# Gated mix of linear attention and a gated ReLU network on one core: six slots for the output row tiles, query weights folded beside key weights, GpSimd's main loop in program order

## The chip, the cores and the metric

The kernel runs on one core of a Trainium2 chip. The metric is the time of one execution on the device in microseconds, the median over runs. The core's engines work in parallel, each through its own list of instructions in order: TensorE (PE in the profile, with its weight loads as PEld), VectorE (DVE), ScalarE (ACT), GpSimd (POOL), and SyncE (SP), which here only issues transfers. Transfers from SP and from GpSimd run on the same 16 DMA engines.

## The reference

Inputs are x (2048 rows of 576), float32. The output is a gate times an attention layer plus the rest of the gate times a feed-forward layer:

```python
qkv = (x @ wqkv).reshape(B, S, 3, H, Dh).transpose(2, 0, 3, 1, 4)    # H = 32 heads of Dh = 18
pq = einsum("bhsd,hdf->bhsf", q, w_phi); pk = einsum("bhsd,hdf->bhsf", k, w_phi)
phi_q = concat([softmax(pq), softmax(-pq)]); phi_k = concat([softmax(pk), softmax(-pk)])
kv = einsum("bhsf,bhsd->bhfd", phi_k, v); z = einsum("bhsf->bhf", phi_k)
o = einsum("bhqf,bhfd->bhqd", phi_q, kv) / (einsum("bhqf,bhf->bhq", phi_q, z) + 1e-6)
a = o @ wo
h = relu(x @ W_gate) * (x @ W_up);  b = h @ W_down                   # F = 4608
g = sigmoid((x * gate_w).sum(-1));  out = g * a + (1 - g) * b
```

## The kernel before

Products are made of float32r parts: a high part that ScalarE rounds (an activation with Copy) and a low part, source minus high, that VectorE subtracts (`split`, L148). So each product costs two or three matmuls.

**Stage 1, to about 31 us.** The values of the first four row tiles (L212 to L245). Then `fold` (L250) multiplies the key weights by the per-head matrix: 25 small matmuls into the three buffers `psf` of the pool `pf`, each group then split by ScalarE and VectorE into `wk_h` and `wk_l`. The weights arrive in tiles `wr` of the pool `raw`, which has four slots in all; a slot is used again when its reader is done, so the order of the loads is also the order in which slots come free.

**Stage 2, folding, to about 60 us.** L397 to L403: `fold` for keys, `load_x(1)` (the next 512 rows of x, tiles `xr`, split into `xh`, `xl`, `x4`), `keys(0)`, `keys(1)`, and `fold` for queries (`wq_h`, `wq_l`). `keys(t)` and `queries(t)` each project a tile of 128 rows by 28 matmuls into one of the two buffers of pool `pp` (`pk`, `pq`). VectorE then takes the maximum and minimum and makes the two differences (`mx`, `mn`, two `e`), which frees the buffer, ScalarE takes the exponential, VectorE the sums `sm` and a reciprocal. For a key tile VectorE scales one half of `e` and GpSimd the other; for a query tile GpSimd scales one half (`e<-r`, L210).

**Stage 3, the main loop, to about 250 us.** L460: for each of the tiles 2 to 13 the keys, the values of the tile (two halves into one PSUM bank `kv`), the queries, the transposes of an earlier query tile (`turn`, `ptr`), and 11 matmuls that add to the attention sums (`kv_step`). From t = 8 GpSimd also makes the first half of the feed-forward operands: `scaled_sums` (L324) loads four blocks `xb`, multiplies them by a row of roots `sb`, subtracts them from one another, and stores seven results to `xt` in device memory. `first_half` is a generator; L471 steps it five times ahead of each tile. Before the change it works on two halves of 256 columns one after the other (eight tiles `xb`). No order is written out in this loop: the tile framework's scheduler places each engine's instructions by its own estimate, within the data dependences.

**Stage 4, attention output, to about 367 us.** Four blocks of 512 rows, the last block first. For block b: `sums` (numerators and denominators, from operands `ph` that `fetch` loads from `eT`), `gather`, `invert` (the denominators `dn`, collected by small transfers on SP, inverted by VectorE, sent on to `kt`), `split_inverse` (GpSimd: `rd`), `divide` (one matmul that spreads `rd`, a VectorE product, then a split into `oh` and `ol`), and the projection: `first_out` for block 0, `project_out` for the others, 14 matmuls for each of five row tiles m. `rows_out` (L756) copies a finished row tile from PSUM to a tile `o` of the pool `tb` and stores it to `att`. For m = 4 the two halves of the bank have to be added: ScalarE copies one half to a tile `b`, VectorE adds the other into `o`. The pool `tb` has four slots, and m = 4 takes two of them; `root_rows` takes one for each of its two calls. Tensor, SP and GpSimd instructions of stages 4 and 5 are held in program order (`in_order`, L54).

**Stage 5, the feed-forward loop, from about 367 us to the end.** 72 units of seven products (`product`, L1091). `second_half` (L1209) makes the other half of the operands, one step per unit, with the same `scaled_sums`.

Of the kernel before, what the change touches and what calls it, by code (L numbers as in the profile page):

```python
# [2 lines left out]

# [13 lines left out]
P = 128  # L17
TB = 512
# [66 lines left out]
def gated_mix_kernel(  # L85
# [77 lines left out]
    def load_x(tb):  # L163
        s = slice(tb * TB, (tb + 1) * TB)
        xh, xl, x4 = x_tiles(tb)
        a = raw.tile([P, 3, TB], F32, name="xr", tag="raw")
        nc.sync.dma_start(a, xT[:, 0:3, s])
        split(xh[:, 0:3], xl[:, 0:3], a)
        b = raw.tile([P, 2, TB], F32, name="xr", tag="raw")
        nc.sync.dma_start(b, xT[:, 3:5, s])  # L170
        split(xh[:, 3], xl[:, 3], b[:, 0])
        split_x4(x4, b[:, 1])
# [77 lines left out]
    def fold(src, dst_h, dst_l, pf):  # L250
        for j0 in range(0, NF, 2):
            n = min(2, NF - j0)
            w = raw.tile([FG, 2, DK], F32, name="wr", tag="raw")
            nc.sync.dma_start(w[:, :n], src[:, j0:j0 + n])
            for j in range(j0, j0 + n):
                c0, gn = FOLDS[j]
                for d0, dn in ((0, 4), (4, 1)):
                    ps = pf.tile([P, 4, P], F32, name="psf")
                    for d in range(dn):
                        nc.tensor.matmul(ps[:, d, :gn], w[:gn, j - j0, (d0 + d) * P:(d0 + d + 1) * P],  # L260
                                         bd[:gn, j, :gn], start=True, stop=True)
                    split(dst_h[:, d0:d0 + dn, c0:c0 + gn], dst_l[:, d0:d0 + dn, c0:c0 + gn],
                          ps[:, :dn, :gn])
# [18 lines left out]
    def keys(t):  # L282
        for _ in key_steps(t):
            pass
# [13 lines left out]
    def whole(steps):  # L298
        for _ in steps:
            pass  # L300
# [16 lines left out]
    def on_all_rows(ps, dst, tb):  # L317

        for i in range(4):
            t = 4 * tb + i  # L320
            nc.tensor.transpose(ps[:, i * P:(i + 1) * P], rs[:, t:t + 1].to_broadcast([P, P]), ident)
        nc.scalar.activation(dst, ps, AF.Copy)

    def scaled_sums(f, hf, b, sb, c0, n):  # L324


        b11, b12, b21, b22 = b
        put = lambda i, a: nc.sync.dma_start(xt[:, hf, i - 1, :, c0:c0 + n], a)
        for i, a in enumerate(b):
            k, t = divmod(i, 2)  # L330
            nc.sync.dma_start(a, xs[:, k, :, (2 * hf + t) * TB + c0:(2 * hf + t) * TB + c0 + n])
        yield
        for i, a in enumerate(b):
            f(out=a, in0=a, in1=sb[:, i % 2, None, :].to_broadcast([P, 3, n]), op=MULT)
            yield
            if i != 1:
                put((1, 0, 2, 3)[i], a)
        for i, o, a, c in ((5, b11, b12, b11), (7, b12, b22, b12), (6, b22, b22, b11), (4, b21, b21, b22)):
            f(out=o, in0=a, in1=c, op=SUB)
            yield  # L340
            put(i, o)
        yield

    def query_steps(t, between=lambda: None, eng=nc.gpsimd):

# [15 lines left out]
    def queries(t):  # L361
        for _ in query_steps(t):
            pass
# [32 lines left out]
    ET = {}  # L396
    with tc.tile_pool(name="pf", bufs=3, space=PSUM, reuse_waits="tile") as pf:  # L397
        fold(wkT, wk_h, wk_l, pf)
        load_x(1)
        nc.sync.dma_start(ident, ident_d)  # L400
        keys(0)
        keys(1)
        fold(wqT, wq_h, wq_l, pf)  # L403
    gate_logits(0)
    gate_logits(1)
    ps_kv = AP.enter_context(tc.tile_pool(name="ps_kv", bufs=1, space=PSUM, reuse_waits="tile"))
# [16 lines left out]
    def operands(tb):  # L423
        PH[tb] = PP[BLOCKS.index(tb) % 2].tile([QK, 4, NQ, P], F32, name="ph")

# [17 lines left out]
            for i in range(0, 5, 2):  # L443
                nc.sync.dma_start(wod[i // 2, :, 10:12 if i < 4 else 11], o[:, 0, i:min(i + 2, 5)].bitcast(F32))

    xw = AR.enter_context(tc.tile_pool(name="xw", bufs=8, **R_))
    WOUT = {}

    def load_out_weights():
# [7 lines left out]
                WOUT[4, k] = w[:, 10 + k % 2], None  # L457

    first_half = iter(())
    for t in range(2, NT - 2):  # L460
        if t in (6, 10):
            load_x(t // 4 + 1)
        if t == 8:
            whole(half_gates(0))
            sb = xw.tile([P, 2, TB], F32, name="sb", bufs=1)
            for i in range(2):
                on_all_rows(pv1.tile([P, TB], F32, name="pg", tag="pv1"), sb[:, i], i)
            halves = [[xw.tile([P, 3, TB // 2], F32, name="xb") for _ in range(4)] for _ in range(2)]
            first_half = chain(*(scaled_sums(pt, 0, halves[c], sb[:, :, c * TB // 2:][:, :, :TB // 2], c * TB // 2, TB // 2)
                                 for c in range(2)))  # L470
        for _ in range(5):  # L471
            next(first_half, None)
        if t == 12:
            for _ in first_half:
                pass
            AR.close()
            pad = RS.enter_context(tc.tile_pool(name="pad", bufs=1, **R_))
            pad.tile([P, 24], F32, name="pad")
            kt_p = RS.enter_context(tc.tile_pool(name="kt_p", bufs=1, **R_))
            kt_ = kt_p.tile([P, 2 * TB], F32, name="kt")  # L480
            gT = kt_[:, TB:]
            kt = kt_[:, :NJ * QK].rearrange("p (g c) -> p g c", g=NJ)
            PP = [RS.enter_context(tc.tile_pool(name="ph0", bufs=1, **R_))]
            operands(BLOCKS[0])
            spread = kt_p.tile([4 * H, 5, P], F32R, name="spread")
            ones = raw.tile([4 * H, 5, P], F32, name="ones", tag="raw")
            nc.sync.dma_start(ones, spread_d)
            nc.gpsimd.tensor_copy(spread, ones)
            load_out_weights()
        keys(t)  # L490
        if t >= 4:
            turn(t - 4, 0)
            values(t, 0)
            turn(t - 4, 1)
            values(t, 1)
        gate_logits(t)
        queries(t - 2 if t < FIRST else t)
        if t >= 4:
            turn(t - 4, 2)
        kv_step(t - 2)  # L500
        if t in (2, 3, 4, 5, 7):
            out_weights((2, 3, 4, 5, 7).index(t))


    def kv_out():
        nc.scalar.activation(kt[:, 4:], kv[1][:, :NJ - 4], AF.Copy)
# [149 lines left out]
    with in_order(tc, nc, nc.tensor, nc.sync, nc.gpsimd):  # L656
# [51 lines left out]
        invert(0)  # L708
        gather(0, 3, 2, 1, 0)
        split_inverse(0)  # L710
        store_turned(FIRST - 2, nc.gpsimd)
        fetch(BLOCKS[2], nc.gpsimd)
        two = pp.tile([P, 2, TB], F32, name="po", tag="pp")
        sums(1, (4,), (kv_bank(0),))
        sums(1, (5,), (kv_bank(1),))
# [29 lines left out]
    xo = ctx.enter_context(tc.tile_pool(name="xo", bufs=3, **L_))  # L745
    xr = ctx.enter_context(tc.tile_pool(name="xr", bufs=2, **L_))
    op_ = BS.enter_context(tc.tile_pool(name="op", bufs=2, **L_))
    tb_ = BS.enter_context(tc.tile_pool(name="tb", bufs=4, **L_))
    XO = {}
    def root_rows(tb):  # L750

# [4 lines left out]
    def rows_out(b, m, ps):  # L756

        n = P if m < 4 else 64
        o = tb_.tile([n, TB], F32, name="o", tag="tb")
        if m < 4:  # L760
            nc.scalar.activation(o, ps, AF.Copy)
        else:
            c = tb_.tile([64, TB], F32, name="b", tag="tb")
            nc.scalar.activation(c, ps[64:], AF.Copy)
            tt(out=o, in0=c, in1=ps[:64], op=ADD)
        nc.sync.dma_start(att[m * P:m * P + n, BLOCKS[b] * TB:(BLOCKS[b] + 1) * TB], o)

    def project_out(b, m):
# [825 lines left out]
```

## Time and profile before

| | |
|---|---|
| three runs | 1623.77, 1625.07, 1628.36 us; median 1625.07 |
| the profiled execution | 1625.07 us, its span 1623.3 us, so 1.8 us lie around the span |
| busy share of the span | PE 98%, PEld 81%, DVE 74%, ACT 34%, POOL 11% |
| granted TensorE clock, mean | 0.991 of full |
| stages by the timeline | values and key weights to 31.6 us, folding to 60.2, main loop to about 250, attention output to 367.0, feed-forward to the end |

A row of the view by windows gives a stretch (start and end in us from the span's start), its length, then for each engine the busy time and the number of instructions, the granted clock, the DMA engines' busy share and GB/s. A row of a timeline gives start, duration, engine, line, operation, output and input tiles with their shapes, how many instructions are merged, and in brackets how long the engine stood idle before and what it waited for. Matmuls overlap, so the recorded duration of one is longer than its step to the next. A row of the view of waits gives who waited for whom, the total, how often, and the longest.

### The profile page before, as it was taken

The page shows a single profiled execution, that of the slowest core. Times are in us where ns is not written, and L with a number is a line of the kernel's source. Part 1 is how long each engine was busy: PE and PEld are TensorE (multiplying, and loading weights), DVE is VectorE, ACT ScalarE, POOL GpSimd, SP SyncE. Part 2 cuts the span into 40 slices and gives each one's busy share as a digit, 9 for nine tenths or more (in the row PEclk, how much of TensorE's full clock was granted, in tenths as well). Part 3 has the DMA queues.
Part 4 walks back from the last instruction along what each step waited for, and adds up shares of the span by engine and source line. Part 5 has one row for each costly group of instructions (what it writes and reads, how often), then busy time and mean ns, then how long its engine had stood idle before and what let it go on. Part 6 is the DMA issues. An engine that isn't in the chain of part 4 may idle for free.

```text
span 1623.3 us, 20196 instructions
## 1 busy us (share of the span) xinstructions
PE 1587.4 (98%) x7823; PEld 1319.7 (81%) x7823; DVE 1195.4 (74%) x1864; ACT 559.9 (34%) x918; POOL 171.7 (11%) x234
## 2 busy tenths in 40 slices
PE   8999999898999999999999999999999999999998
PEld 8899996466888888888888887788888888888887
DVE  4898775368777877877777777677777777767777
ACT  4344335345323323323323324232323223232331
POOL 0128311200000000000000002111111111111110
PEclk9899999999999999999999999999999999999999
DMA  8254405557675566566555434643434334353432
GB/s 269 66 187 135 147 17 148 185 202 281 227 259 222 195 224 248 189 225 230 194 197 194 186 120 152 223 167 134 180 129 180 147 148 166 132 192 131 165 149 73
DMA packets 71562, 284.59 MB, mean 175 GB/s; under 512 B 7018, under 2 KB 25962, under 8 KB 62764
## 3 DMA queue, kind: packets, MB, share of 16 engines
q1 hardware_dynamic: 69020, 273.30, 46.5%
q0 software_dynamic: 1872, 8.97, 1.9%
q8 instruction: 61, 1.00, 0.3%
q10 hardware_dynamic: 576, 1.05, 0.2%
q14 instruction: 33, 0.27, 0.0%
HBM read 172.67 MB, written 109.21 MB: 174 GB/s over the span
## 4 chain that ended last, share of the span: by engine, by line
PE 88%; DVE 4%; DMA 3%; POOL 2%; ACT 1%; issue 1%; SPq 0%; DVEq 0%; POOLq 0%; ACTq 0%
PE cx L1091 27%; PE ca L1091 13%; PE pd L1131 12%; PE pd L1154 10%; PE cy L1091 7%; PE kv L176 4%; PE pq L176 3%; PE pk L176 2%; PE pm L1131 2%; PE pm L1154 2%; PE pw L176 1%; PE kv L416 1%; DMA wdr<-wd 1%; PE pv L238 1%; DMA ph<-eT 1%
## 5 line engine op out<-in xcount | busy, mean ns | idle before, releaser
L1198 ACT ACTIVATE hh<-g 128x512 fp32r<-128x512 f32 x195 | 120.0, 624 | 459.0 <-DVE g L1248 289.7
L1169 DVE TENSOR_TENSOR ac<-pd,ac 128x512 f32<-128x512 f32 x238 | 163.9, 689 | 146.3 <-PE pd L1154 146.1
L1091 PE MATMUL cx<-xo,ws 128*128 128x512 f32 x1008 | 253.3, 391 | 4.2 <-ACT g L1252 4.2
L1091 PE MATMUL cx<-xo,wb 128*128 128x512 f32 x1008 | 250.9, 392 | 5.2 <-DVE u L1373 3.5
L1091 PE MATMUL ca<-xo,ws 128*128 128x512 f32 x1008 | 252.0, 389 | 0.7 <-DMA ws<-wsd 0.7
L1091 PEld LDWEIGHTS cx<-xo,wb 128*128 128x128 f32 x1008 | 189.2, 189 | 47.3 <-DVE u L1373 4.3
L1091 PEld LDWEIGHTS cx<-xo,ws 128*128 128x128 f32 x1008 | 189.5, 188 | 44.8 <-ACT g L1252 5.4
L1091 PEld LDWEIGHTS ca<-xo,ws 128*128 128x128 f32 x1008 | 189.1, 188 | 40.3 <-issue 1.1
L1131 PE MATMUL pd<-hh,wd 128*128 128x512 f32 x576 | 200.7, 389 | 0.0
L1154 PE MATMUL pd<-hh,wd 128*128 128x512 f32 x476 | 185.2, 389 | 0.0
L1137 DVE TENSOR_TENSOR ac<-pd,ac 128x512 f32<-128x512 f32 x144 | 99.0, 688 | 106.6 <-PE pd L1131 103.1
L1203 DVE TENSOR_TENSOR hl<-g,hh 128x512 fp32r<-128x512 f32 x195 | 136.3, 699 | 1.9 <-ACT hh L1198 0.2
L1252 ACT ACTIVATE g<-cx 128x512 f32<-128x512 f32 x144 | 85.0, 590 | 127.1 <-PE cx L1091 127.0
L1091 PE MATMUL cy<-xo,wb 128*128 128x512 f32 x504 | 126.6, 391 | 0.0
L1131 PEld LDWEIGHTS pd<-hh,wd 128*128 128x128 f32 x576 | 108.1, 188 | 22.5
L1054 ACT ACTIVATE wd<-wdr 128x384 fp32r<-128x384 f32 (+1 forms) x106 | 62.3, 606 | 153.4 <-DMA wdr<-wd 153.4
L1131 PE MATMUL pd<-hl,wd 128*128 128x512 f32 x288 | 112.1, 389 | 1.0 <-ACT xo L823 1.0
L1091 PEld LDWEIGHTS cy<-xo,wb 128*128 128x128 f32 x504 | 95.2, 189 | 20.0
L1154 PEld LDWEIGHTS pd<-hh,wd 128*128 128x128 f32 x476 | 89.3, 188 | 18.6
L1154 PE MATMUL pd<-hl,wd 128*128 128x512 f32 x238 | 92.6, 389 | 0.0
L807 POOL TENSOR_TENSOR xo<-xr,xo 32x512 fp32r<-32x512 f32 x5 | 8.2, 1638 | 656.2 <-DVE xo L807 648.4
L1057 DVE TENSOR_TENSOR wd<-wdr,wd 128x384 fp32r<-128x384 f32 (+1 forms) x106 | 69.4, 669 | 5.7 <-ACT wd L1054 5.7
(250 smaller groups left out, 2577.8 us busy)
## 6 DMA issues: line engine op xcount, KB each, us to landing
wsd<-ws SPq DMA_DIRECT2D x34, 1280.0 KB
ws<-wsd SPq DMA_DIRECT2D x34, 1280.0 KB
wbd<-wb SPq DMA_DIRECT2D x34, 960.0 KB
wb<-wbd SPq DMA_DIRECT2D x34, 960.0 KB
wr<-wgu SPq DMA_DIRECT2D x36, 768.0 KB
wdr<-wd SPq DMA_DIRECT2D x36, 576.0 KB
xt<-xb SPq DMA_DIRECT2D x28, 384.0 KB
xb<-xs SPq DMA_DIRECT2D x16, 384.0 KB
```

The source lines that it names most:

```text
L176: nc.tensor.matmul(ps, w, m, start=i == 0, stop=i == len(pairs) - 1)
L238: nc.tensor.matmul(pv[i][c], m, w_[:, k, cs], start=k == 0 and n == 0, stop=k == 4 and n == 1)
L1054: nc.scalar.activation(o[:, 0], a, AF.Copy)
L1057: tt(out=o[:, 1], in0=a, in1=o[:, 0].bitcast(F32), op=SUB)
L1091: nc.tensor.matmul(ps, w, v, start=first and m == 0, stop=m == len(pairs) - 1, skip_group_check=True)
L1131: nc.tensor.matmul(ps, w, v, start=k == 0 and (i < 2 or first), stop=k == len(mms) - 1 and (i < 2 or last), skip_group_check=True)
L1137: tt(out=a, in0=ps, in1=a, op=ADD)
L1154: mm = lambda ps, w, v, a, z: nc.tensor.matmul(ps, w, v, start=a, stop=z, skip_group_check=True)
L1169: tt(out=a, in0=ps, in1=a, op=ADD)
L1198: nc.scalar.activation(h, src, AF.Copy)
L1203: tt(out=l, in0=src, in1=h.bitcast(F32), op=SUB)
L1252: nc.scalar.activation(a, ps, AF.Copy)
```

## The change

1. `tb` gets six slots instead of four, and `rows_out` for m = 4 copies the half straight to `o` and adds in place, so that five row tiles take five slots instead of six.
2. The query weights are loaded and folded right behind the first key tile; `load_x(1)` comes after them.
3. The main loop stands inside `in_order` for GpSimd. `first_half` works on whole blocks (four loads of 768 KB instead of eight of 384 KB, seven stores instead of fourteen); each operation is split into two pieces of 256 columns, and `bits` steps it at three places of a tile (2, 1 and 1 pieces) instead of five times at its head. Its loads are tied behind the SP instruction that was traced last at t = 8.
4. `fetch(BLOCKS[2])` goes ahead of `store_turned(FIRST - 2)` on GpSimd's queue.
5. `scaled_sums` loses its last `yield`, so `second_half` takes one unit less per half.

```diff
-    def scaled_sums(f, hf, b, sb, c0, n):
+    def scaled_sums(f, hf, b, sb, c0, n, pieces=1):
...
+        parts = [slice(i * n // pieces, (i + 1) * n // pieces) for i in range(pieces)]
...
         for i, a in enumerate(b):
-            f(out=a, in0=a, in1=sb[:, i % 2, None, :].to_broadcast([P, 3, n]), op=MULT)
-            yield
+            for c in parts:
+                f(out=a[:, :, c], in0=a[:, :, c], in1=sb[:, i % 2, None, c].to_broadcast([P, 3, n // pieces]), op=MULT)
+                yield
             if i != 1:
                 put((1, 0, 2, 3)[i], a)
         for i, o, a, c in ((5, b11, b12, b11), (7, b12, b22, b12), (6, b22, b22, b11), (4, b21, b21, b22)):
-            f(out=o, in0=a, in1=c, op=SUB)
-            yield
+            for p in parts:
+                f(out=o[:, :, p], in0=a[:, :, p], in1=c[:, :, p], op=SUB)
+                yield
             put(i, o)
-        yield
...
         fold(wkT, wk_h, wk_l, pf)
-        load_x(1)
         nc.sync.dma_start(ident, ident_d)
         keys(0)
+        fold(wqT, wq_h, wq_l, pf)
+        load_x(1)
         keys(1)
-        fold(wqT, wq_h, wq_l, pf)
...
-    xw = AR.enter_context(tc.tile_pool(name="xw", bufs=8, **R_))
+    xw = AR.enter_context(tc.tile_pool(name="xw", bufs=4, **R_))
...
+    def bits(n):
+        for _ in range(n):
+            next(first_half, None)
+    with in_order(tc, nc, nc.gpsimd):
+        for t in range(2, NT - 2):
...
+                first_half = scaled_sums(pt, 0, [xw.tile([P, 3, TB], F32, name="xb") for _ in range(4)], sb, 0, TB, 2)
+                with after(tc, nc, nc.sync, last_of(nc, nc.sync)):
+                    next(first_half)
...
+            keys(t)
+            if t >= 4:
+                turn(t - 4, 0)
+                values(t, 0)
+                bits(2)
+                turn(t - 4, 1)
+                values(t, 1)
+            gate_logits(t)
+            bits(1)
+            queries(t - 2 if t < FIRST else t)
+            if t >= 4:
+                turn(t - 4, 2)
+            kv_step(t - 2)
+            bits(1)
...
+        fetch(BLOCKS[2], nc.gpsimd)
         store_turned(FIRST - 2, nc.gpsimd)
-        fetch(BLOCKS[2], nc.gpsimd)
...
-    tb_ = BS.enter_context(tc.tile_pool(name="tb", bufs=4, **L_))
+    tb_ = BS.enter_context(tc.tile_pool(name="tb", bufs=6, **L_))
...
-            c = tb_.tile([64, TB], F32, name="b", tag="tb")
-            nc.scalar.activation(c, ps[64:], AF.Copy)
-            tt(out=o, in0=c, in1=ps[:64], op=ADD)
+            nc.scalar.activation(o, ps[64:], AF.Copy)
+            tt(out=o, in0=o, in1=ps[:64], op=ADD)
```

Since a scheduler places the instructions of stages 1 to 3, the built programs show what the edits move. In the changed program line numbers of these stages are one lower or a few higher than before.

First, SP's queue at the folding. The names: `wr` are weights to fold (wkT for keys, wqT for queries), `xb` the feed-forward blocks, `xr` the rows of x for `load_x(1)`, `wor` output weights. Before:

```order
L254 DMA wr<-wkT 126x1280 x2
L254 DMA wr<-wkT 126x640
L331 DMA xb<-xs 128x3x256 x8
L167 DMA xr<-xT 128x3x512
L170 DMA xr<-xT 128x2x512
L254 DMA wr<-wqT 126x1280 x2
L254 DMA wr<-wqT 126x640
```

Now:

```order
L253 DMA wr<-wkT 126x1280 x2
L253 DMA wr<-wkT 126x640
L253 DMA wr<-wqT 126x1280 x2
L253 DMA wr<-wqT 126x640
L166 DMA xr<-xT 128x3x512
L169 DMA xr<-xT 128x2x512
L436 DMA wor<-wo 128x640 x2
```

The eight block loads have left this place, the query weights follow the key weights at once, and the rows of x come after them.

Second, VectorE at the same place, from the end of the key weights on (`wk_l`): `mx`, `mn`, `e` belong to a projected tile, `wq_l` are the low parts of folded query weights, `xl` and `x` of the rows of x. Before:

```order
L150 TENSOR_TENSOR wk_l<-psf,wk_h 128x72
L150 TENSOR_TENSOR xl<-xr,xh 128x1536
L150 TENSOR_TENSOR xl<-xr,xh 128x512
L161 TENSOR_TENSOR x_364<-xr,x_364 64x512
L195 TENSOR_REDUCE mx<-pk 128x32
L196 TENSOR_REDUCE mn<-pk 128x32
L200 TENSOR_TENSOR e<-pk,mx 128x32x18
L201 TENSOR_TENSOR e<-mn,pk 128x32x18
```

Now:

```order
L149 TENSOR_TENSOR wk_l<-psf,wk_h 128x72
L194 TENSOR_REDUCE mx<-pk 128x32
L195 TENSOR_REDUCE mn<-pk 128x32
L199 TENSOR_TENSOR e<-pk,mx 128x32x18
L200 TENSOR_TENSOR e<-mn,pk 128x32x18
L149 TENSOR_TENSOR wq_l<-psf,wq_h 128x4x126
L149 TENSOR_TENSOR wq_l<-psf,wq_h 128x126
L149 TENSOR_TENSOR wq_l<-psf,wq_h 128x4x126
L204 TENSOR_REDUCE sm<-e 128x64
```

VectorE turns to the first key tile without the rows of x in between, and then to the query weights.

Third, GpSimd in the main loop from t = 8 on: `e<-e,sm` is the scaling of a key tile, `e<-e,r` of a query tile, the `xb` rows are pieces of the first half. Before:

```order
L334 TENSOR_TENSOR xb<-xb,sb 128x768 x5
L210 TENSOR_TENSOR e<-e,r 128x32x18
L339 TENSOR_TENSOR xb<-xb 128x768
L334 TENSOR_TENSOR xb<-xb,sb 128x768
L339 TENSOR_TENSOR xb<-xb 128x768
L334 TENSOR_TENSOR xb<-xb,sb 128x768
L339 TENSOR_TENSOR xb<-xb 128x768
L334 TENSOR_TENSOR xb<-xb,sb 128x768
L210 TENSOR_TENSOR e<-e,sm 128x32x18
L339 TENSOR_TENSOR xb<-xb 128x768 x3
L210 TENSOR_TENSOR e<-e,r 128x32x18
```

Now:

```order
L335 TENSOR_TENSOR xb<-xb,sb 128x3x256 x3
L209 TENSOR_TENSOR e<-e,r 128x32x18
L335 TENSOR_TENSOR xb<-xb,sb 128x3x256
L209 TENSOR_TENSOR e<-e,sm 128x32x18
L335 TENSOR_TENSOR xb<-xb,sb 128x3x256 x3
L209 TENSOR_TENSOR e<-e,r 128x32x18
L335 TENSOR_TENSOR xb<-xb,sb 128x3x256
L209 TENSOR_TENSOR e<-e,sm 128x32x18
```

A scaling now stands behind at most three pieces; before, eleven pieces with one scaling among them stood ahead of the key scaling shown.

More of the change, by code (lines that the diff above doesn't have):

```diff
@@ L1 @@
 from contextlib import ExitStack, contextmanager
-from itertools import chain
 import concourse.bass as bass
@@ L459, in gated_mix_kernel @@
     first_half = iter(())
[L460 to L471, printed above, removed]
-            next(first_half, None)
[L473 to L502, printed above, removed]
```

26 lines of the change are left out of this document (added).

## The prediction

> **What bounds the kernel now.** I read the page's engine shares first, then the view by windows, then waits and timelines where TensorE falls short.
>
> ```profile
> PE 1587.4 (98%) x7823; PEld 1319.7 (81%) x7823; DVE 1195.4 (74%) x1864; ACT 559.9 (34%) x918; POOL 171.7 (11%) x234
> ```
>
> TensorE carries the time, so an edit is worth what it takes from TensorE's idle time, or from time at a low clock.
>
> ```profile
> 31.64:60.18 28.54, 24.04 (x135) 22.72 (x133) 22.04 (x33) 9.30 (x16) 2.38 (x2) 0.76 0.28 81
> 60.18:84.60 24.42, 24.42 (x219) 23.28 (x218) 23.31 (x34) 9.82 (x14) 5.12 (x4) 1.00 0.24 82
> 84.60:98.66 14.06, 14.06 (x118) 13.57 (x118) 13.46 (x20) 6.52 (x11) 3.79 (x3) 1.00 0.71 246
> ...
> 142.14:156.21 14.07, 14.07 (x118) 13.58 (x118) 10.18 (x16) 6.40 (x10) 14.07 (x9) 1.00 0.26 87
> 156.21:172.05 15.84, 14.32 (x118) 13.60 (x119) 14.44 (x17) 5.92 (x10) 12.83 (x9) 1.00 0.79 238
> 299.65:311.70 12.05, 5.46 (x11) 2.48 (x9) 5.02 (x8) 3.42 (x6) 0.00 (x0) 0.72 0.63 227
> 366.98:383.25 16.27, 11.61 (x43) 8.77 (x42) 15.93 (x22) 10.49 (x15) 0.00 (x0) 0.90 0.75 257
> ```
>
> Columns are PE, PEld, DVE, ACT, POOL busy, then the clock. Four stretches lose time: the folding (idle, and a clock of 0.76), one main-loop tile that takes 15.84 us where its neighbour with the same 118 matmuls takes 14.07, the output stage around 300 us, and the entry to the feed-forward loop. The rows at 60.18 and 84.60 carry a warning: right behind the folding VectorE is nearly as full as TensorE.
>
> **Folding.**
>
> ```profile
> 37.70 3.39 PE L260 MATMUL psf<-bd,wr 126*128 126x126 f32 x18 [2.33 <-DMA wr<-wqT]
> ...
> 45.95 0.49 PE L260 MATMUL psf<-bd,wr 126*128 126x126 f32 x2 [0.70 <-DVE wq_l L150]
> 47.41 1.48 PE L260 MATMUL psf<-bd,wr 126*128 126x126 f32 x10 [0.97 <-DVE wq_l L150]
> 49.24 0.61 PE L176 MATMUL pq<-wq_h,xh 128*128 128x288 f32 x1 [0.36 <-ACT wq_h L149]
> 50.00 4.12 PE L260 MATMUL psf<-bd,wr 126*128 126x126 f32 x18
> ```
>
> TensorE first waits 2.33 us for query weights, then 2.03 in three pieces for their splits, which stand behind key tiles on VectorE; the clock is low after each. Lost from 31.64 to 60.18: 4.4 idle, plus 24.04 x (1 - 0.76) = 5.8, together 10.2 us.
>
> ```profile
> 14.20 8.89 SPq L331 DMA_DIRECT2D xb<-xs  x8
> 24.36 0.37 SPq L167 DMA_DIRECT2D xr<-xT  x1
> 27.14 0.37 SPq L170 DMA_DIRECT2D xr<-xT  x1
> 28.61 8.46 SPq L254 DMA_DIRECT2D wr<-wqT  x3
> ```
>
> The query loads were issued at 28.61 and later, behind 3.1 MB of blocks. Now they take the slots that rows of x took at 24.36 and 27.14, with no blocks ahead, so they can land before the first key tile ends on TensorE (31.6), and VectorE takes their splits between its key work. Not all 10.2 us come back: VectorE was busy 22.04 of 28.54, 23.31 of 24.42 and 13.46 of 14.06, so it had 6.5 + 1.1 + 0.6 = 8.2 us to spare up to 98.66, and the same work must be done there. Some of that spare stays, for ScalarE's exponentials and the rows of x, which now land later; I leave 0.7 (the 1.7 spare of the last two rows shows it can run that tight). **Gain 7.5.** Ends: 10.2, if VectorE's lag is caught up behind 98.66, and 3.2, if the clock falls once more: of the 5.8 I put 1.5 down to the stretch from 37.70 (its eighteen records took 3.39 us; at the pace of the ten at 47.41 they take 2.7, and key matmuls behind them ran slow for a while) and 4.3 to the one from 50.00 (4.12 for eighteen). Late next is VectorE; behind it wait TensorE's next key or query tile, for a buffer of two. The two output-weight splits on ScalarE stand ahead of the second key tile's exponential; their load is covered by that tile's VectorE work.
>
> The Trainium skill's TensorE: Matmul & The Clock Gate, section HAM oscillation, says that only TensorE gaps of more than about 3.4 us bring the clock down. This trace doesn't agree: the clock was low behind 2.33 us, and behind 2.03 us in three pieces. By the page the folding's low end would be 7.5 and not 3.2.
>
> **Main loop, GpSimd in order.**
>
> ```profile
> PE ptr L373 <- POOL e L210: 1.5, 1, 1.5
> L334 POOL TENSOR_TENSOR xb<-xb,sb 128x768 f32<-128x768 f32 x8 | 14.6, 1844 | 4.4 <-ACT sb L322 4.4
> ```
>
> Before, a query scaling stood behind a run of pieces, and TensorE's transposes waited for it. Now at most three pieces, 3 x 1.84 = 5.5 us, stand ahead of a scaling whose reader comes two tiles (28 us) later. Work on GpSimd is the same, sixteen pieces, 29.5 us over four tiles of 56. The gain is the long tile's excess, 15.84 - 14.07: **1.7** (ends 0 and 1.8). The loads are now late, about at t = 8, but the DMA share at 142.14 is 0.26, so there is room.
>
> **Output rows.** First stall, block 0:
>
> ```profile
> 295.42 0.59 ACT L761 ACTIVATE o<-kv 128x512 f32<-128x512 f32 x1
> 303.49 0.59 ACT L764 ACTIVATE b<-pw 64x512 f32<-64x512 f32 x1 [7.48 <-DMA att<-o]
> ```
> ```profile
> 305.96 0.68 DVE L765 TENSOR_TENSOR o<-b,pw 64x512 f32<-64x512 f32 x1 [9.13 <-DMA att<-o]
> ```
> ```profile
> 299.65 0.40 PE L176 MATMUL kv<-oh,wo 128*128 128x512 f32 x1
> 304.66 0.69 PE L176 MATMUL kv<-oh,wo 128*128 128x512 f32 x1 [4.61 <-ACT oh L611]
> 307.29 0.80 PE L176 MATMUL kv<-ol,wo 128*128 128x512 f32 x1 [1.95 <-DVE ol L612]
> ```
>
> Four slots are full with four stores under way; ScalarE's fifth copy and VectorE's add wait for them, the splits `oh` and `ol` stand behind, and TensorE waits for those, then runs slowly. With six slots (five used by block 0, the sixth by the next row tile, the seventh asked for behind the next `sums`, about 303.5, when the first store has landed) nothing waits there. From 299.65 the eleven remaining matmuls took 12.05 us up to 311.70; fourteen take 3.22 below, so eleven take 2.5, and TensorE would be done about 302.1: 9.6 us sooner. What is late next is the chain of block 2's denominators:
>
> ```profile
> 314.22 3.22 PE pw L176 x14
> 317.43 1.87 PE po L548 x8
> 319.30 0.38 PE kv L608
> ```
> ```profile
> 268.00 3.41 SPq L554 DMA_DIRECT2D dn<-R  x4
> ```
> ```profile
> 281.74 0.95 DVE L585 RECIPROCAL dn<-dn 128x128 f32<-128x128 f32 x1 [6.57 <-DMA dn<-R]
> ```
> ```profile
> 311.63 0.63 SPq L587 DMA_DIRECT2D kt<-dn  x1
> ```
> ```profile
> 313.92 0.60 POOL L595 CAST rd<-kt 32x512 fp32r<-32x512 f32 x1 [20.12 <-DMA kt<-dn]
> 314.61 1.28 POOL L596 TENSOR_TENSOR rd<-kt,rd 32x512 fp32r<-32x512 f32 x1
> ```
>
> TensorE needs `rd` at the spread matmul (319.30), 7.6 us behind 311.70, so now at 309.7. In block 1 the `dn` transfers, issued by 271.4 beside GpSimd's fetches, landed only at 281.7. Block 2's would be issued near 300, beside the same kind of fetches, which still held a store until 305.96. I take 306 for the landing; the reciprocal and its product (1.2), the transfer to `kt` (2.3 from its issue to the cast) and GpSimd's 1.95 give 311.5, a wait of 1.8, and about 0.8 for a clock that may drop behind it: **gain 7.0** (ends 4.0, if `dn` lands 10 us after its issue as in block 1 and the clock drops, and 9.6).
>
> The skill's DMA: Bandwidth & Descriptors, section Queues, rings and completion order, says that each DMA engine takes turns between queues packet by packet; a small transfer then need not wait for a long one on another queue. The row at 281.74 speaks against it. By the page the wait would be gone and the gain 9.6.
>
> Second stall, block 3:
>
> ```profile
> 362.76 0.60 ACT L761 ACTIVATE o<-pw 128x512 f32<-128x512 f32 x1 [5.45 <-DMA att<-o]
> 363.26 1.48 ACT L839 ACTIVATE ws<-wr 128x1536 fp32r<-128x1536 f32 x1
> ```
> ```profile
> 360.68 0.56 DVE L863 TENSOR_TENSOR wr<-wr 128x384 f32<-128x384 f32 x1
> ```
>
> With six slots that copy finds one stored long before. The weight sums `ws` behind it still need VectorE's L863, done at 361.24, so ScalarE comes 2.0 sooner, and VectorE, which sets the entry to the feed-forward loop (15.93 of 16.27 busy at 366.98), moves with it: **gain 2.0** (ends 1.0 and 3.7, with the low clock gone too). The add in place costs what it did.
>
> **The rest.**
>
> ```profile
> 282.65 1.90 PE L548 MATMUL po<-ph,kvm 108*64 108x512 f32 x6 [1.16 <-DMA ph<-eT]
> ```
> ```profile
> PE cx L1091 <- DMA wb<-wbd: 1.7, 1, 1.7
> ```
>
> The fetch ahead of the store lands one store sooner, but the reciprocal at 281.74 holds the next division anyway: **0.2** (ends -0.3 and 1.2). The lost `yield` moves loads by one unit in the feed-forward loop, where transfers are covered by full TensorE work: **0**, at worst one more wait of 1.7 like the one shown.
>
> **Sum**: 7.5 + 1.7 + 7.0 + 2.0 + 0.2 = 18.4. The profiled execution took 1625.07, also the median: 1625.07 - 18.4 = 1606.7, say **1607**.
>
> **Rivals.**
> 1. The clock falls again in the folding: its gain is 3.2, and the time 1611. For it: it fell behind pieces under 1 us. Against it: VectorE's work is spread. 0.13.
> 2. The denominators' chain takes most of the first stall: gain 4.0, time 1610. For it: block 1's 10 us. Against it: the fetches end sooner after the issue. 0.13.
> 3. Small transfers pass the fetches, and only then is nothing left of the stall: 9.6, time 1604. For it: `kt` landed within 2.3 us at 313.92; against it: the row at 281.74. 0.09. The second page above speaks for this one.
> 4. The change doesn't do what it says: VectorE's order, which the scheduler chose, takes the folding's gain, and the slots were not what the stores wait for; time about 1624. 0.04.
> 5. Slower: GpSimd in order makes every scaling wait for block loads. A scaling has 28 - 4 x 1.84 = 20.7 us before TensorE reads it; each us that a block lands later than that after GpSimd asks for it costs one, and 18.4 are undone from 39 us on. SP would have to hold the loads behind stores for that long; beside full engines the `dn` transfers above took 10 us. Time about 1629. 0.08, more than the rows give, since SP's new order isn't shown.
>
> **Numbers.** The forecast, 1607, has 0.53; cases 1 to 3 make 0.88 faster with it, 0.04 within 0.3% (about 5 us, what a measurement of this kernel can tell from no change), 0.08 slower. The likeliest case by itself runs from 1603 to 1611; the range 1600 to 1614 takes in cases 1 to 3.
>
> **What would show it.** Right: the query fold starts without a wait for `wr<-wqT` and the clock stays at 1.00 between 30 and 55 us; no wait of ACT or DVE for `att<-o`; the tile around 156 takes 14.1; the span is shorter by 7 to 8 us at 90 us and by 9 at 250. Wrong: VectorE waits on the rows of x, TensorE waits on `pk` buffers through several tiles, `rd` ends a wait over 4 us, or GpSimd waits for `xb<-xs` beyond 20 us.

## The result, and the profile after

The changed kernel takes 1607.36 us (median of 6 runs, 1605.71 to 1612.24), the kernel before 1626.55 us (6 runs, 1623.77 to 1628.36): a ratio of 0.9887, with a 95% interval of 0.9871 to 0.9904, 19.2 us less. The profiled execution took 1607.92 us, its span is 1605.9 us (before 1623.3) and its mean granted clock 0.997 (before 0.991).

To see where the 17.4 us between the two spans lie, both traces are cut at the same instructions of TensorE, so that each stretch holds the same matmuls. The cuts of the kernel before are the first product of the key weights (21.29), two transposes of the main loop (96.92 and 198.35), three spread matmuls of the attention output (269.15, 297.96, 325.24), and the products behind the last long wait at the entry of the feed-forward loop (383.25). "After again" is a second profiled execution of the changed kernel; it comes up below.

| stretch, us | before | after | difference | after again | difference | forecast |
|---|---|---|---|---|---|---|
| start, values | 21.29 | 23.67 | +2.38 | 22.09 | +0.80 | 0 |
| folding and the tiles behind it | 75.63 | 66.69 | -8.94 | 67.29 | -8.34 | -7.5 |
| main loop, tiles with GpSimd's pieces | 101.43 | 99.35 | -2.08 | 99.30 | -2.13 | -1.7 |
| end of the loop, block 3's first sums | 70.80 | 70.57 | -0.23 | 70.58 | -0.22 | 0 |
| up to the last part of block 0 (the fetch) | 28.81 | 27.91 | -0.90 | 27.85 | -0.96 | -0.2 |
| first stall | 27.28 | 22.95 | -4.33 | 24.47 | -2.81 | -7.0 |
| second stall, entry of the loop | 58.01 | 56.06 | -1.95 | 56.04 | -1.97 | -2.0 |
| feed-forward loop | 1240.05 | 1238.70 | -1.35 | 1237.48 | -2.57 | 0 |
| sum | 1623.30 | 1605.90 | -17.4 | 1605.10 | -18.2 | -18.4 |

The rows of the profile after for these stretches (view by windows; PE, PEld, DVE, ACT, POOL busy with instructions, clock, DMA share, GB/s):

```profile
23.67:90.36 66.69, 64.89 (x521) 61.59 (x522) 59.49 (x95) 28.05 (x53) 9.85 (x8) 1.00 0.36 115
90.36:189.71 99.35, 99.35 (x829) 95.76 (x828) 81.21 (x124) 43.93 (x69) 51.59 (x32) 1.00 0.55 191
...
260.28:288.19 27.91, 26.86 (x108) 15.49 (x106) 14.50 (x27) 12.95 (x23) 6.31 (x11) 1.00 0.74 211
288.19:311.14 22.95, 19.30 (x77) 11.43 (x75) 5.34 (x9) 7.86 (x14) 2.94 (x4) 0.93 0.56 203
311.14:367.20 56.06, 50.43 (x206) 37.28 (x204) 42.22 (x58) 31.22 (x43) 3.76 (x3) 1.00 0.63 220
```

TensorE is busy in all 99.35 us of the main loop's row, and the clock is 1.00 everywhere but in the first stall's stretch. From the end of the first key tile to a tile boundary, the piece for which the prediction reckons with VectorE's time, the same view gives:

```profile
34.03:92.03 58.00, 56.50 (x469) 53.30 (x468) 56.78 (x83) 24.63 (x39) 9.85 (x8) 1.00 0.35 115
```

The folding, in TensorE's timeline and in SP's:

```profile
34.03 2.17 PE L259 MATMUL psf<-bd,wr 126*128 126x126 f32 x18
...
37.88 1.50 PE L259 MATMUL psf<-bd,wr 126*128 126x126 f32 x12
```
```profile
26.75 4.56 SPq L253 DMA_DIRECT2D wr<-wqT  x3
38.30 0.41 SPq L166 DMA_DIRECT2D xr<-xT  x1
```

The brackets for `wr<-wqT` and `wq_l` are gone, and eighteen products take 2.17 us instead of 3.39 and 4.12. What is left of the first stall, in the timelines of TensorE, VectorE, GpSimd and SP:

```profile
293.41 1.90 PE L556 MATMUL po<-ph,kvm 108*64 108x512 f32 x6 [1.07 <-issue]
...
299.04 1.94 PE L556 MATMUL po<-ph,kvm 108*64 108x512 f32 x8
303.56 0.68 PE L616 MATMUL kv<-rd,spread 64*64 64x512 f32 x1 [2.58 <-POOL rd L604]
...
304.94 1.63 PE L175 MATMUL kv<-oh,wo 128*128 128x512 f32 x3
```
```profile
297.89 0.95 DVE L593 RECIPROCAL dn<-dn 128x128 f32<-128x128 f32 x1 [6.49 <-DMA R<-og]
```
```profile
282.37 0.56 POOL L431 DMA_DIRECT2D ph<-eT  x1 [2.71 <-DMA eT<-et]
282.91 1.12 POOL L789 DMA_DIRECT2D xr<-xt  x2
301.56 0.60 POOL L603 CAST rd<-kt 32x512 fp32r<-32x512 f32 x1 [17.53 <-DMA kt<-dn]
```
```profile
288.93 1.59 SPq L562 DMA_DIRECT2D dn<-R  x2
290.70 3.19 SPq L578 DMA_DIRECT2D R<-og  x2
299.24 0.63 SPq L595 DMA_DIRECT2D kt<-dn  x1
```

TensorE, ScalarE and VectorE no longer wait for `att<-o` there: block 0's products run through. But the reciprocal of block 2 stands until 297.89 for small transfers (`dn<-R`) issued by 290.52. Its bracket names a transfer of `R`, which by the program it does not read. TensorE waits 2.58 us for `rd`, and the matmuls behind run slowly (three in 1.63 us; three of the same kind at 311.57, at full clock, in 0.96). The bracket "issue" at 293.41 is a wait whose cause that view does not give. The transfer that it needs is the last part of block 3's operands, issued at 282.37 behind a store; the view of transfers gives 11.0 us for its landing, which makes 293.4:

```profile
xr<-xt POOLq DMA_DIRECT2D x2, 768.0 KB, 13.8
...
ph<-eT POOLq DMA_DIRECT2D x1, 594.0 KB, 11.0
```

The same view gives 13.8 us for the two loads of feed-forward operands issued at 282.91: they land at about 297, just ahead of the reciprocal.

### The profile page after: what moved, and what is told of

Read it like the earlier page. It is cut to its first block, busy times and chain, and to the rows that moved or that the text cites. A ratio compares the mean times of both kernels' runs of the same rounds, so it can differ in the third digit from the quotient of the medians.

```text
span 1605.9 us, 20175 instructions
## 1 busy us (share of the span) xinstructions
PE 1580.5 (98%) x7823; PEld 1314.5 (82%) x7823; DVE 1192.4 (74%) x1864; ACT 559.9 (35%) x918; POOL 171.3 (11%) x234
## 4 chain that ended last, share of the span: by engine, by line
PE 91%; DMA 3%; DVE 3%; ACT 1%; issue 1%; POOL 0%; SPq 0%; ACTq 0%; DVEq 0%; POOLq 0%
PE cx L1098 28%; PE ca L1098 13%; PE pd L1138 12%; PE pd L1161 10%; PE cy L1098 7%; PE kv L175 4%; PE pq L175 3%; PE pk L175 3%; PE pm L1138 2%; PE pm L1161 2%; PE kv L417 1%; DMA dn<-R 1%; PE ptr L374 1%; PE pv L237 1%; DMA wdr<-wd 1%; PE pw L175 1%
```

## Experiments

Each kernel ran on one chip beside the kernel before. Its medians there were 1625.59 us for the four runs on the folding and the slots alone, 1626.39 for the changed kernel again, five slots, the `yield` and the blocks alone, and 1625.67 for the other four; differences are against these. The changed kernel stood 19.2 us under the kernel before, and 18.65 in its second measurement.

**The folding: order, or blocks out of the way?** First, edit 2 alone on the kernel before:

```diff
-        load_x(1)
         nc.sync.dma_start(ident, ident_d)
         keys(0)
+        fold(wqT, wq_h, wq_l, pf)
+        load_x(1)
         keys(1)
-        fold(wqT, wq_h, wq_l, pf)
```

> Before with edit 2 alone (query weights loaded and folded behind the first key tile, rows of x after them); the eight block loads stay where the scheduler puts them, between the key and the query weights on SP. Theory A, the place of the fold on VectorE and in the slots of `raw` is what counts: the whole folding gain of about 8.9 us (what the changed kernel shows between 21 and 98 us), so about 1617.7 against 1626.6, no wait for wr<-wqT, clock 1.00 through the folding. Theory B, 3.1 MB of blocks ahead on the queue are what made the weights late: TensorE still waits some 2 us for wr<-wqT and its clock falls behind it, gain 4 to 5, about 1622.

Measured: 1622.04 us, 3.55 less, ratio 0.9978 (0.9962 to 0.9993). TensorE and SP in its trace:

```profile
34.43 2.25 PE L260 MATMUL psf<-bd,wr 126*128 126x126 f32 x18 [2.05 <-DMA wr<-wqT]
```
```profile
14.05 9.34 SPq L331 DMA_DIRECT2D xb<-xs  x8
24.94 4.57 SPq L254 DMA_DIRECT2D wr<-wqT  x3
```

Theory B's wait is there: the weights were asked for at 24.94, behind 3.1 MB of blocks issued up to 23.39, and TensorE still stood 2.05 us for them. But the clock did not fall behind it, and the folding's stretch is 69.17 us, 6.5 less than before's. The total shows only 3.55 of it. In the profiled execution the main loop takes 1.8 us back (see the next run), and the stretch of the fetch 3.7: it lasts 32.52 us instead of 28.81. There TensorE waits 1.83 us for `ph` instead of 1.16, and this time the clock falls behind the wait, so that six products take 3.14 us instead of 1.90. TensorE's timeline, and the stretch by windows:

```profile
279.31 3.14 PE L548 MATMUL po<-ph,kvm 108*64 108x512 f32 x6 [1.83 <-DMA ph<-eT]
```
```profile
265.09:297.61 32.52, 29.85 (x107) 16.94 (x106) 12.64 (x25) 11.77 (x21) 6.31 (x11) 0.90 0.77 199
```

Neither loss lies in the folding, so this total says less about the two theories than the stretch does.

Edit 2 with the eight loads tied to tile 8 (the kernel before otherwise):

```diff
-            first_half = chain(*(scaled_sums(...) for c in range(2)))
+            parts = [scaled_sums(...) for c in range(2)]
+            with after(tc, nc, nc.sync, last_of(nc, nc.sync)):
+                for p in parts:
+                    next(p)
+            first_half = chain(*parts)
```

> Before with edit 2 and with the eight block loads tied to tile 8, as the change does it; GpSimd's order stays the scheduler's. Both theories: the folding gain of about 8.9, so about 1617.7 plus or minus what the main loop makes of the later blocks (the long tile of 15.84 us may stay, move or go: 0 to 1.8 less). Theory A says that it equals the run with edit 2 alone within 1.5 us up to 98 us, theory B that it is 4 us shorter there.

Measured: 1619.44 us, 6.15 less, ratio 0.9963 (0.9953 to 0.9973). The stretch is 66.89 us, as in the changed kernel, 2.3 shorter than with edit 2 alone (theory A allowed 1.5, theory B asked for 4); no wait for `wr<-wqT`. The main loop's stretch grew to 103.15 us (before 101.43): GpSimd's long run now makes TensorE wait 2.27 us at one transpose, and the clock falls behind that (in both of these runs). So the folding gives up about 2 us to the main loop as long as GpSimd's order is the scheduler's.

The other side: the loads tied, the folding's order old (same edit, without edit 2):

> Before with the eight block loads tied to tile 8 and nothing else; the folding keeps its old order. What the changed kernel without edit 2 showed (72.3 us from the first key-weight product to the tile boundary behind the folding, where before took 75.6): about 3 us less there, so 1622 to 1623.5, no wait for wr<-wqT, but waits for wq_l. Rival: the blocks only matter together with the new order (75 us again): 1626.

Measured: 1623.59 us, 2.80 less by the medians, but a ratio of 0.9990 (0.9980 to 1.0000), whose interval reaches no change. The stretch is 70.95 us, 4.7 less, with no wait for `wr<-wqT` and 2.7 us for `wq_l`. The stretch of the fetch is again long, 32.45 us, with a wait of 1.81 us and the low clock behind it. And the changed kernel with the old folding order:

```diff
+        load_x(1)
         nc.sync.dma_start(ident, ident_d)
         keys(0)
-        fold(wqT, wq_h, wq_l, pf)
-        load_x(1)
         keys(1)
+        fold(wqT, wq_h, wq_l, pf)
```

> The changed kernel with the folding's old order (rows of x, both key tiles, then the query weights); the blocks stay out of the way. Theory A: the folding's gain is gone, about 1607.4 + 8.9 = 1616; TensorE waits for wr<-wqT or for wq_l as before and the clock falls. Theory B: only half is gone, about 1611 to 1612, and no wait for wr<-wqT.

Measured: 1611.42 us, 14.17 under before, so 4.5 to 5 of the gain are lost; the stretch is 72.31 us, with 2.8 us for `wq_l` and none for `wr<-wqT`. Neither theory holds whole. Theory A falls, since the blocks count too. Theory B's 1611 to 1612 came out here, but its 1622 for edit 2 alone came with the help of a loss elsewhere, and the clock that it expected to fall behind the wait for the weights did not. In the stretch itself the order brings 6.5 us alone, 4.1 with the blocks away (70.95 to 66.89) and 5.0 to 5.6 in the changed kernel; the blocks bring 4.7 alone and 2.3 behind the order. So both count, the order for more. Together they bring 8.7. What is taken from before's 75.63 is uncertain by 2 us: the run on the slots, below, has the same folding and took 73.38, against which the order brings 4.2, the blocks 2.4 and both 6.5. Whether the two simply add up therefore stays open. The totals, 2.80 and 3.55 against 6.15 for both, do not settle it, since the profiled executions of the two single runs carry the low clock at the fetch and that of both together does not.

**GpSimd's order.** The changed kernel with the main loop's `in_order` for no engine:

```diff
-    with in_order(tc, nc, nc.gpsimd):
+    with in_order(tc, nc):
```

> The changed kernel with GpSimd's main loop left to the scheduler (all else stays: whole blocks, pieces, the loads tied to tile 8). Theory: a query scaling stands behind a run of pieces again and TensorE's transposes wait for it: a tile of 15.8 to 17.9 us instead of 14.07, so 1.7 to 3.8 more, 1609.1 to 1611.2. Rival: the finer pieces alone prevent it: within 1 us of the changed kernel.

Measured: 1614.20 us, 11.47 under before: 7.2 to 7.7 us lost, more than either theory said. TensorE's timeline at that place:

```profile
157.91 1.10 PE L374 MATMUL ptr<-ident,e 128*108 128x128 f32 x4 [6.22 <-POOL e L209]
...
159.06 0.45 PE L175 MATMUL kv<-wv_l,xh 128*128 128x294 f32 x1
159.30 0.45 PE L175 MATMUL kv<-wv_h,xl 128*128 128x294 f32 x1
...
160.76 0.30 PE L175 MATMUL kv<-wv_h,xl 128*128 128x294 f32 x1
160.89 0.30 PE L175 MATMUL kv<-wv_h,xh 128*128 128x294 f32 x1
```

One tile takes 21.77 us (from 146.04 to 167.81), 7.7 over the usual 14.07: 6.22 of waiting and 1.5 at a low clock, in which one matmul follows the next by 0.245 us instead of 0.135. Finer pieces on whole blocks do not help without the order; they made it worse.

**The slots.** Edit 1 alone on the kernel before:

```diff
-    tb_ = BS.enter_context(tc.tile_pool(name="tb", bufs=4, **L_))
+    tb_ = BS.enter_context(tc.tile_pool(name="tb", bufs=6, **L_))
...
-            c = tb_.tile([64, TB], F32, name="b", tag="tb")
-            nc.scalar.activation(c, ps[64:], AF.Copy)
-            tt(out=o, in0=c, in1=ps[:64], op=ADD)
+            nc.scalar.activation(o, ps[64:], AF.Copy)
+            tt(out=o, in0=o, in1=ps[:64], op=ADD)
```

> Before with six slots and the addition in place, nothing else. Theory A, what the changed kernel's trace shows of this edit (first stall 4.3 net of the wait for rd, second stall 2.0): 6.3 less, about 1620.3, no wait for att<-o, and a wait of 2 to 3 us for rd at block 2's spread matmul. Rival, the wait for rd comes from another edit (the fetch ahead of the store, or GpSimd's order): no wait for rd, 9.6 + 2.0 = 11.6 less, about 1615.

Measured: 1618.45 us, 7.14 less, ratio 0.9958 (0.9946 to 0.9970). First stall 4.04 less, second 1.95 less, and a wait of 3.6 us for `rd`: theory A. The rest lies in the folding, whose stretch was 73.38 us here although nothing of it was edited: the same instructions differ there by about 2 us between two executions.

The changed kernel with four slots, and likewise with five:

```diff
-    tb_ = BS.enter_context(tc.tile_pool(name="tb", bufs=6, **L_))
+    tb_ = BS.enter_context(tc.tile_pool(name="tb", bufs=4, **L_))
```

> The changed kernel with four slots in the pool `tb` (the addition stays in place, so a block needs five). Theory: the slots carry the gain; the fifth row tile of block 0 waits for the first store again, and block 3's too, so 4.3 + 2.0 come back: about 1613.7, with waits of ScalarE for att<-o. Rival: the slot that the addition in place saves is already enough (the fifth row tile asks for a slot late): within 1 us of the changed kernel, 1607 to 1608.5.

> The changed kernel with five slots in `tb`. By the prediction's reading block 0 takes five and the row tile asked for next finds the first store landed by then (in the changed kernel it is copied at 299.15 for m = 1, 292.37 for m = 0, and block 0's first store was issued at 283): if stores land within 9 us, five is enough for the first stall but m = 0 at 292.4 waits up to 1 us; block 3's rows come every 3.2 us and a store there takes less than 16, so nothing waits: within 1 us of the changed kernel. Rival: stores take 10 us or more beside the fetches and ScalarE waits for att<-o at 292: 1 to 3 us more.

Measured with four: 1612.43 us, 13.24 under before, so 5 to 6 are lost, as the theory said. In the view of waits of its output stage:

```profile
ACT o L771 <- DMA att<-o: 8.0, 1, 8.0
ACT o L769 <- DMA att<-o: 5.8, 1, 5.8
```

With five: 1607.73 us, and 1607.74 for the changed kernel on the same chip. ScalarE does wait once (ScalarE's timeline), for block 0's first store, issued at 281.45:

```profile
293.03 0.60 ACT L769 ACTIVATE o<-kv 128x512 f32<-128x512 f32 x1 [3.88 <-DMA att<-o]
```

That is the rival's wait, but it costs nothing: TensorE waits 4.4 us for `rd` a little later, and 4.3 with six slots. So the saved slot and one more carry the gain; the sixth is spare as long as the wait for `rd` is there.

**The fetch, and the last `yield`.** The changed kernel with edit 4, and with edit 5, undone:

```diff
-        fetch(BLOCKS[2], nc.gpsimd)
         store_turned(FIRST - 2, nc.gpsimd)
+        fetch(BLOCKS[2], nc.gpsimd)
```

> The changed kernel with the store ahead of the fetch on GpSimd's queue again (edit 4 undone). The prediction's term: 0.2 more, 1607.6. What the changed kernel's trace shows between the spread matmuls at 268.73 and 288.19 says 1.1 more, 1608.5: a wait of about 1.2 us of TensorE for ph<-eT in front of block 2's sums, of which 0.2 is covered by another wait.

Measured: 1608.23 us, 17.44 under before, so 1.2 to 1.8 lost, within what can be told from no change. Its profile shows waits that were not there, or shorter:

```profile
PE kv L616 <- POOL rd L604: 4.6, 1, 4.6
...
PE po L556 <- DMA ph<-eT: 2.1, 1, 2.1
```

The stretch of the fetch is 1.64 us longer than in the changed kernel's first execution. That is on the side of the trace's 1.1 rather than the 0.2, but not settled by the times.

```diff
                 yield
             put(i, o)
+        yield
```

> The changed kernel with the last `yield` of scaled_sums back (edit 5 undone). Prediction's term 0: from the entry of the feed-forward loop to the end 1237 to 1240 us as in all nine profiled runs, time within 1 us of the changed kernel. Rival: the 1.35 us by which the changed kernel's profiled execution was shorter there came from it: 1.4 us more.

Measured: 1606.57 us, 1.2 less than the changed kernel on the same chip, again within no change; its feed-forward loop took 1237.87 us. So edit 5 is worth nothing that shows. What moves that loop most is the clock at its entry. Over all kernels it ran from 1237.1 to 1240.05 us. In six profiled executions the clock stays at 1.00 behind the entry's last long wait, and the loop takes 1237.1 to 1237.9 us; in the other eight it falls there, and the loop takes 1238.7 to 1240.05. The changed kernel has one of each, with nearly the same wait. TensorE's timeline and the first 8 us of the loop, "after", then "after again":

```profile
367.20 5.08 PE L1098 MATMUL cx<-xo,wb 128*128 128x512 f32 x14 [2.94 <-DVE u L1380]
367.62 3.46 PE L1098 MATMUL cx<-xo,wb 128*128 128x512 f32 x14 [2.92 <-DVE u L1380]
```
```profile
367.20:375.20 8.00, 8.00 (x28) 6.45 (x29) 6.72 (x11) 3.51 (x5) 0.00 (x0) 0.79 1.00 420
367.62:375.62 8.00, 8.00 (x35) 6.65 (x36) 6.83 (x11) 4.26 (x7) 0.00 (x0) 1.00 1.00 421
```

Seven products fewer in 8 us are about 1.5 us. The kernel before has 0.79 there too, so the 1.35 us between it and "after" have another source, which stays open.

**The start.** The changed kernel once more:

> The changed kernel once more. In its profiled execution the first key-weight product began at 23.67 us; in the nine others, of kernels that are the same up to there, at 21.3 to 22.1. Theory: chance at the start (first loads, clock), not the change: now 21.3 to 22.1 again, and the terms from there on repeat within 0.5 us: 66.7 us to the tile boundary behind the folding, long tile gone, wait for rd 2 to 4.6. Rival: the change's order costs 2 us at the start: 23 or more again.

Measured: 1607.74 us, ratio 0.9896 (0.9880 to 0.9912). The first product of the key weights came at 22.09, and in the two executions measured beside it at 21.99 and 21.67. So 23.67 was chance. The terms repeat within 0.6 us (table above) but for the first stall, where the wait for `rd` is 4.3 instead of 2.58 us, and the feed-forward loop with its clock.

**What is left of the first stall.** The two operand loads go behind the denominators' chain:

```diff
         fetch(BLOCKS[3], nc.gpsimd)
-        load_operand(0, 0, nc.gpsimd)
-        load_operand(0, 1, nc.gpsimd)
...
         split_inverse(2)
+        load_operand(0, 0, nc.gpsimd)
+        load_operand(0, 1, nc.gpsimd)
```

> The changed kernel with the two loads of the first feed-forward operands (768 KB each, GpSimd's queue) moved behind block 2's split of the inverse. Theory: the small transfers of block 2's denominators land only when these two loads are through (about 297.8, 7.3 us after the last was issued), so without them they land within 2 us, VectorE inverts at about 292, TensorE does not wait for rd (2.6), its clock does not fall behind that (1.6), and the last part of block 3's operands lands before TensorE asks for it (1.1): 5.2 less, about 1602.2. Rival 1: the five stores of block 0's row tiles, on SP's own queue, hold the small transfers: the wait for rd stays above 1.5 us and only the 1.1 is won, about 1606.3. Rival 2: the operands are now late for ScalarE's split at 312 and the loss moves to the entry of the feed-forward loop: 1607 or more.

Measured: 1601.61 us (1600.28 to 1603.65), ratio 0.9851 (0.9830 to 0.9873), faster than both kernels: 24.06 under before. VectorE, TensorE and GpSimd in its trace, and its row by windows:

```profile
293.12 0.95 DVE L593 RECIPROCAL dn<-dn 128x128 f32<-128x128 f32 x1 [3.49 <-DMA att<-o]
```
```profile
291.38 1.90 PE L556 MATMUL po<-ph,kvm 108*64 108x512 f32 x6 [0.82 <-issue]
...
296.98 1.94 PE L556 MATMUL po<-ph,kvm 108*64 108x512 f32 x8
298.85 0.45 PE L616 MATMUL kv<-rd,spread 64*64 64x512 f32 x1
```
```profile
298.66 1.14 POOL L789 DMA_DIRECT2D xr<-xt  x2
```
```profile
286.41:304.87 18.46, 17.64 (x78) 10.30 (x76) 5.35 (x9) 7.74 (x14) 4.06 (x6) 1.00 0.61 195
```

The spread matmul follows without a wait, the clock is 1.00, and the stretch is 18.46 us, 8.8 under before's 27.28. The loads, issued 16 us later, land within 6.5 us, in time for ScalarE. The reciprocal came at 293.12, not 292: 4.3 us behind the last small transfer's issue (SP's 287.15 plus 1.71), still beside the fetch and the stores. The theory's sum holds, but for the wait of 1.1, of which 0.8 stayed.

## Why the prediction was right, step by step

The time, 1607.4 against a forecast of 1607, came out right partly by luck: errors of 1 to 4 us cancelled. The first stall gave 2.7 to 4.2 us less than forecast; the folding, measured against the same trace as the forecast, gave 0.8 to 1.4 more, the fetch 0.7 more, and the feed-forward loop, with no term, 1.4 to 2.6; the start took 0.8 to 2.4 back.

- **Folding, 7.5.** Measured 8.3 to 8.9 against the profiled execution of before, and 6.1 to 6.7 against the execution with 73.38; the term lies between. The mechanism holds on both counts that the prediction named, the loads with no blocks ahead and VectorE's splits between its key work; the runs show that both count, the second for more. VectorE did run tight. In the piece that the prediction reckoned with, 67.02 us before with VectorE busy 58.81, it keeps 1.2 us to spare where 0.7 was forecast (row at 34.03 above). The piece is 9.0 us shorter and not 7.5, since VectorE's work in it is not "the same work" but 2.0 us less, 83 instructions instead of 86. Rival 1 did not come: clock 1.00.
- **Main loop, 1.7.** 2.1, of which 1.69 is the long tile: it takes 14.08 us now (147.52 to 161.60). GpSimd waits nowhere for `xb<-xs`, so rival 5's mechanism is absent. What the prediction missed is that the edits depend on each other: with the new folding the long tile would have grown to 17.9 us, and with whole blocks to 21.77. The order is worth 7.2 to 7.7 us in the kernel it came with.
- **First stall, 7.0.** 4.3 and 2.8; this is the term that was mis-sized. The stores stop nobody, as forecast, and the chain of `dn`, `kt` and `rd` is late next, as forecast. The step that failed is "I take 306 for the landing". On the old kernel's time axis (9.77 us later at the spread matmuls ahead) the reciprocal began at 307.7, since the small transfers waited for the two operand loads and not for a store and a fetch that end early. The wait was 2.58 instead of 1.8, the low clock cost 1.6 instead of 0.8 (from 303.56 to 311.14 it took 7.58 us, at full clock 6.0), and 1.07 for the last part of `ph` was not in the sum at all: 9.6 - 2.58 - 1.6 - 1.07 = 4.35. In the second execution the wait was 4.27, beyond the 4 us that the prediction named as a sign of being wrong, and the gain of 2.8 lies under the term's low end of 4.0. So rival 2's price came in this term; its time, 1610, did not, as other terms gave more. Its "against", that the fetches end sooner after the issue, was wrong.
- **Rival 3**, small transfers that pass the long ones. From their last issue to the reciprocal took 1.4 us in the kernel before (308.87 to 310.29; the two loads had landed at about 307), 4.3 with the fetch and stores in flight, 7.4 with the two loads as well. They do not pass freely, so the turns by packet that the Trainium skill's DMA: Bandwidth & Descriptors describes in its section Queues, rings and completion order were not enough to keep them short here.
- **Second stall, 2.0.** 1.95 and 1.97, with the clock at 1.00.
- **Fetch, 0.2.** 0.9 and 0.96, close to its upper end: the wait of 1.16 us went and the reciprocal did not take its place. Where the clock falls behind that wait the edit saves more: the two single runs on the folding, which lack it, took 4.5 to 4.6 us longer in this stretch than the changed kernel.
- **Rival 4**, that the change does not do what it says, is out: each of edits 1 to 3, undone (edit 1 in its slots, edit 3 in GpSimd's order), cost 4.5 us or more.
- **Outside the terms.** The start, +2.38 and +0.80, chance; the feed-forward loop, -1.35 and -2.57, of which the 1.2 between the two executions go with the clock at its entry, and 1.35 stay unexplained.

## What to carry to other kernels

When a stall goes, look at what is in flight at that moment and not only at which instruction is late next: the remaining 5 us here were two loads that landed at 297 for a reader at 312, and issuing them 16 us later cost the next stage 0.6 us at most. A scheduler's order around a slow helper engine is worth pinning before other stages are made faster, since its harm changes with them. Executions of one kernel differ by 2 us in single stages, so compare stages over several traces before giving each a price. And read every stage of a run before its total is laid to the edit: edit 2 alone shortened its own stage by 6.5 us and showed 3.55, mostly because a wait elsewhere grew by 0.7 us and the clock fell behind it.

## What the runs showed of the hardware

**The clock behind a wait.** How long TensorE waits does not settle by itself whether the clock falls. In the fourteen traces no wait up to 1.75 us that stood alone lowered it, and all thirteen from 3.47 to 6.22 us did. Between them it goes either way: waits of 1.81 and 1.83 us and all seventeen from 2.10 to 2.72 lowered it, waits of 2.05 and 2.09 did not, and the one of 2.92 to 3.08 us at the entry of the feed-forward loop did so in three executions and not in six, in the changed kernel once each way (rows under the last `yield`). What decides there no run shows. Nor is one long wait needed: in the folding of before the clock was low behind three pieces of 0.70, 0.97 and 0.36 us within 4 us.

TensorE's timeline of the run with edit 2 alone shows a drop's start, at a transpose of the main loop:

```profile
156.18 0.65 PE L373 MATMUL ptr<-ident,e 128*108 128x128 f32 x4 [2.27 <-POOL e L210]
156.59 0.38 PE L176 MATMUL kv<-wv_h,xh 128*128 128x294 f32 x1
156.80 0.32 PE L176 MATMUL kv<-wv_l,xh 128*128 128x294 f32 x1
156.94 0.43 PE L176 MATMUL kv<-wv_h,xl 128*128 128x294 f32 x1
157.16 0.45 PE L176 MATMUL kv<-wv_h,xh 128*128 128x294 f32 x1
...
159.62 0.45 PE L176 MATMUL kv<-wv_l,x 128*128 128x294 f32 x1
```

The first matmuls are at full pace; the slow ones begin at about 156.9, 3 us after the wait began, and last some 3 us. Behind 6.22 us (shown with GpSimd's order) they begin at once and end 2.8 us later. In both, the tile lost 1.5 us beyond the wait itself (17.88 - 14.07 - 2.27 and 21.77 - 14.07 - 6.22), so there the length of the wait does not set the price. It is not always 1.5: behind the 1.83 us at the fetch in the same run the clock was low for some 6 us, and the stretch lost 3.0 beyond the longer wait (32.52 - 28.81 - 0.67).

The Trainium skill's TensorE: Matmul & The Clock Gate, section HAM oscillation, names gaps of TensorE of more than about 3.4 us as what to avoid. The traces agree for the waits from 3.47 us up, and show that shorter ones are not safe.
